# Attention with memory slots and a top-1 mixture of experts: where the expert gate is worked out

## The chip, the cores and the metric

The kernel runs on one core of a Trainium2 chip. The metric is the device time of one execution in microseconds; of several executions the median is given.

## The reference

An attention whose keys and values are first folded into 32 memory slots per head makes 4608 rows x of 512 numbers. Each row goes to the one of 8 experts with the largest logit, through a two-layer network with 1024 hidden units, and the result is scaled by a gate of two factors: the row's largest softmax probability and the sigmoid of its output logit for that expert.

```python
a = softmax(phi, over the sequence)              # 8 batches x 8 heads x 576 x 32
k_m, v_m = a^T k, a^T v                          # 32 x 64 per head
x = softmax(q k_m^T / 8) v_m                     # 4608 x 512
logits = x @ w_gate
e_idx = np.argmax(logits, axis=1)
probs = np.exp(logits - logits.max(-1)); probs /= probs.sum(-1) + 1e-9
eom = 1.0 / (1.0 + np.exp(-(x @ w_output_gate)))
for e in range(8):
    h = np.maximum(x[mask] @ w1[e], 0.0)
    out[mask] = gate_w[mask, None] * eom[mask, e, None] * (h @ w2[e])
```

The exponential of the largest logit minus itself is 1, so the gate of a row is 1 / ((sum of exp(logit - max) + 1e-9) x (1 + exp(-output logit))).

## The kernel before

**Attention and rows.** The attention runs over four pairs of batches. Each row of x goes to a scratch array `xs` in HBM as four quarters of 144 numbers: 128 values, and 16 partial logits (8 for the experts, 8 for the output gate) that belong to the two heads of that quarter. The sum of a row's four sets of 16 is its logits.

**Ranking.** Once per pair `rank` (L932) gives each row its expert and its place among the rows of that expert: maximum, comparisons, a product with a triangular matrix on TensorE (L981 to L985), and one-hot rows on GpSimd (L1014). Beside these steps it works out the gates of the pair's 1152 rows: logit minus maximum on GpSimd (L957), an exponential (L967), the chosen output logit (L966) and its sum (L973), the sum of the exponentials (L987), the exponential of the negated output logit (L988), two additions, a product, a reciprocal (L993 to L1004) and a copy to 16 columns (L1006). Four DMAs of SyncE (L1008, L1011) then write the gate over the partial logits of every quarter of the rows in `xs`. For the second pair these DMAs wait in a list and are issued from hooks. `rank` is a generator: its steps are taken one by one, among the steps of other work.

**Expert slots.** The rows of an expert are worked off in slots: five slots of three blocks of 128 rows that are gathered as whole rows (slots 0 to 4; 0 and 1 run while the attention still goes on), then nine "quart" slots, in turn of three blocks and of two (five and four of them), whose rows are gathered quarter by quarter, so that a quarter of a row lies on each group of 32 partitions. Slots of single blocks stand behind a condition on the counts and don't run with these inputs. A gather of GpSimd (L542) brings the rows into `xg` (three buffers).

`several` (L1281) computes one slot. First half: for each of 4 weight tiles u and 2 column blocks j a group of 12 matmuls (three-block slot) or 8 (two-block) into a PSUM bank, with x as a rounded part xh and a rest xl, weights split likewise; ScalarE and VectorE take each bank out. In a three-block slot these are L1307 and L1308. In a two-block slot they are a copy (ScalarE L1310), an addition (VectorE L1311), then per u a relu (ScalarE L1315) and two differences (VectorE L1318). After j = 0 and at the end of each u stands a call of `hook`, 8 in a slot. Second half: turns (u, k) of matmuls L1340, one y bank for each block k, and at the last u `finish_y` scales y by the gate on ScalarE (L1275) and scatters it (L1276).

The next slot's operands are made in the second half of the slot before, in five calls of `turn_x`, c = 0 to 4: for quart slots a transpose on VectorE (L1118), the rounded part on ScalarE (L1136) and the rest on VectorE (L1137). A slot's first group of matmuls needs all four chunks: it goes through chunk 0 to 3, with xh, xl, xh for each. Where `turn_x` has c = 0 for a quart slot, four small copies on ScalarE (L1111) also bring the gates, which lie in the gathered rows, to the partitions of y as `gx`. Whole slots take the gate from `xg` in place.

Between all this VectorE and ScalarE split weights: L587 rounds a 128x1024 tile on ScalarE, L602 makes the rest on VectorE, two tiles for every tile used up, through a ring of ten tiles in the quart slots. Instructions of an engine run in the order in which the program issues them.

Of the kernel before, what the change touches and what calls it, by code (L numbers as in the profile page):

```python
# [9 lines left out]
F32 = mybir.dt.float32  # L10
# [3 lines left out]
AF = mybir.ActivationFunctionType  # L14
# [4 lines left out]
P = 128  # L19
# [3 lines left out]
NCH = 9  # L23
# [48 lines left out]
def attention_moe(tc, phiT, kv, qT, wgo, wall, out):  # L72
# [3 lines left out]
    with contextlib.ExitStack() as ctx:  # L76
# [854 lines left out]

        def rank(bp, lg):  # L932

            t0 = bp * 2 * S
            lt = lg[:, :, 0:E]
            lo = lg[:, :, E:2 * E]
            b3 = [P, NCH, E]
            cs = slice(bp * NCH, (bp + 1) * NCH)
            lm = rt.tile([P, NCH], F32, name="lm")
            w1_ = rt.tile(b3, F32, name="w1_")  # L940
            w2_ = rt.tile(b3, F32, name="w2_")
            w3_ = rt.tile(b3, F32, name="w3_")
            pm = rt.tile([P, NCH], F32, name="pm")
            zs = rt.tile([P, NCH], F32, name="zs")
            gd = rt.tile([P, NCH], F32, name="gd")
            oc = rt.tile([P, E], F32, name="oc")
            rki = rt.tile([P, NCH], I32, name="rki")
            ri = rt.tile([P, NCH], I32, name="ri")
            row = rt.tile([P, NCH], F32, name="row", bufs=2)
            gt = rt.tile([P, NCH, XQ - P], F32, name="gt")  # L950
            oh = ohg[:, cs]
            dscb = desc[:].unsqueeze(1).to_broadcast(b3)
            lmb = lm[:].unsqueeze(2).to_broadcast(b3)
            V.tensor_reduce(lm[:], lt, axis=AX.X, op=ALU.max)
            yield
            V.tensor_tensor(w1_[:], lt, lmb, ALU.is_ge)
            G.tensor_tensor(w2_[:], lt, lmb, ALU.subtract)  # L957
            yield
            V.tensor_tensor(w1_[:], w1_[:], dscb, ALU.mult)
            yield  # L960
# [2 lines left out]
            V.tensor_tensor(oh, dscb, pm[:].unsqueeze(2).to_broadcast(b3), ALU.is_equal)  # L963
            yield
            V.tensor_reduce(oc[:], oh.rearrange("p c e -> p e c"), axis=AX.X, op=ALU.add)
            V.tensor_tensor(w3_[:], oh, lo, ALU.mult)  # L966
            A.activation(w2_[:], w2_[:], AF.Exp)  # L967
            yield
            if bp:
                V.tensor_tensor(ohcs[bp][:], ohcs[bp - 1][:], oc[:], ALU.add)  # L970
            else:
                V.tensor_copy(ohcs[bp][:], oc[:])
            V.tensor_reduce(zs[:], w3_[:], axis=AX.X, op=ALU.add)  # L973
            yield

            def rest():
                yield from take_pr()
                yield from hold(LATE["pe"])

                pr = ps_r.tile([P, NCH, E], F32, name="pr")  # L980
                T.matmul(pr[:], strict[:], oh, start=True, stop=False)  # L981
                if bp:
                    T.matmul(pr[:], ones_b[:], ohcs[bp - 1][:].unsqueeze(1).to_broadcast(b3), start=False, stop=False)
                for c in range(1, NCH):
                    T.matmul(pr[:, c:], ones_b[:], oh[:, 0:NCH - c], start=False, stop=(c == NCH - 1))  # L985
                yield
                V.tensor_reduce(gd[:], w2_[:], axis=AX.X, op=ALU.add)  # L987
                A.activation(zs[:], zs[:], AF.Exp, scale=-1.0)  # L988
                yield
                yield from hold(LATE["dve"])  # L990
                V.tensor_tensor(w1_[:], oh, pr[:], ALU.mult)
                taken.clear()
                V.tensor_scalar(gd[:], gd[:], 1e-9, None, ALU.add)  # L993
                yield
                with nc.allow_low_precision("whole numbers"):
                    V.tensor_reduce(rki[:], w1_[:], axis=AX.X, op=ALU.add)
                V.tensor_scalar(zs[:], zs[:], 1.0, None, ALU.add)
                yield
                V.tensor_scalar(ri[:], rki[:], 127, None, ALU.bitwise_and)
                V.tensor_scalar(jg[:, cs], rki[:], 7, None, ALU.arith_shift_right)  # L1000
                V.tensor_tensor(gd[:], gd[:], zs[:], ALU.mult)
                yield
                V.tensor_copy(row[:], ri[:])  # L1003
                V.reciprocal(gd[:], gd[:])  # L1004
                yield
                V.tensor_copy(gt[:], gd[:].unsqueeze(2).to_broadcast([P, NCH, XQ - P]))  # L1006
                def gates_out(b):
                    nc.sync.dma_start(  # L1008
                        xs[t0 + b * S:t0 + b * S + 512, P:XQ].rearrange("(c p) d -> p c d", p=P),
                        gt[:, 4 * b:4 * b + 4])  # L1010
                    nc.sync.dma_start(xs[t0 + b * S + 512:t0 + b * S + 576, P:XQ], gt[64 * b:64 * b + 64, 8])  # L1011

                def one_hot(c):
                    G.tensor_scalar(Aw[:, bp * NCH + c], iota_row[:], row[:, c:c + 1], None, ALU.is_equal)  # L1014

                if bp == 1 and "open" not in env:
                    kept.extend(functools.partial(gates_out, b) for b in range(2))
                    singly.extend(functools.partial(one_hot, c) for c in range(NCH))
                else:
                    for b in range(2):  # L1020
                        gates_out(b)
                    for c in range(NCH):
                        one_hot(c)
                        if c % 3 == 2:
                            yield
                ranked.append(bp)
# [71 lines left out]
        def turn_x(z, c):  # L1098
# [4 lines left out]
            if c == 0:  # L1103
                z["x"] = (mo.tile([P, 4, 3 * P], F32R, name="xh"),
                          None if nb == 2 else mo.tile([P, 4, 3 * P], F32R, name="xl"))
                if z["quart"]:
                    z["xt"] = {}
                    z["g"] = env["xt"].tile([P, 3], F32, name="gx")
                    for b in range(4):
                        k = nb - (nb == 2 and b > 1)  # L1110
                        A.copy(z["g"][32 * b:32 * b + 32, 0:k], xg[0:32, 0:k, XQ * b + P])  # L1111
            xh, xl = z["x"]
            if z["quart"]:

# [20 lines left out]
                pt = pt[:, 0:n]  # L1135
            A.copy(xh[:, c, 0:n], pt)  # L1136
            V.tensor_tensor(xl[:, c, 0:n], pt, xh[:, c, 0:n].bitcast(F32), ALU.subtract)  # L1137

        NT = 5 * NBP
        deferred = []  # L1140
# [124 lines left out]
        def finish_y(z, k, py):  # L1265
            y = mo.tile([P, DM], F32, name="y", bufs=2)
            n = P
            if (z["nb"], k) == (2, 1):

                n = 64  # L1270
                ya = env["xt"].tile([64, DM], F32, name="ya", bufs=1)
                A.copy(ya[:], py[64:128])
                V.tensor_tensor(ya[:], py[0:64], ya[:], ALU.add)
                py = ya[:]
            A.activation(y[0:n], py[0:n], AF.Copy, scale=z["g"][0:n, k:k + 1] if z["quart"] else z["xg"][:, k, P:P + 1])  # L1275
            G.indirect_dma_start(  # L1276
                out=out, out_offset=bass.IndirectOffsetOnAxis(ap=z["idx"][1][0:n, z["q0"] + k:z["q0"] + k + 1], axis=0),
                in_=y[0:n], in_offset=None, bounds_check=NTOK - 1, oob_is_err=False)

        def several(i, st, nxt, hook):  # L1280


            z = order[i]
            nb, x, h = z["nb"], z["x"], []
            n_ = nb * P
            for u in range(4):
# [34 lines left out]
                if nb == 3:  # L1321
                    st.done(PUMP[0])
                hook()
            py = [bank([DM], "ps") for _ in range(nb)]

            turns = [(u, k) for u in range(4, 8) for k in range(nb)]
# [24 lines left out]
        def single(i, st, nxt):  # L1351
# [15 lines left out]
            for u in range(4):  # L1367
# [12 lines left out]
                    turn_h(0)  # L1380
                if u < 3:
                    st.done(PUMP[1])
            for c in range(5):
                nxt(c)
            turn_h(1)
# [131 lines left out]
```

## Time and profile before

| | |
|---|---|
| median of 3 executions | 546.48 us (546.12 to 997.22) |
| the profiled execution's own time | 548.27 us |
| its span, first to last instruction | 546.5 us |
| mean granted TensorE clock | 0.974 |
| busy: TensorE, VectorE, ScalarE, GpSimd | 508.1, 353.6, 288.1, 239.5 us |
| DMA | 123.54 MB in 42062 packets, of these 10320 under 512 B |

The profiled execution took 1.8 us more than the median and 1.77 us more than its own span. The engine names in the rows are PE for TensorE, PEld for its weight loads, DVE for VectorE, ACT for ScalarE, POOL for GpSimd and SP for SyncE. Each line of the timeline has the start in us, the duration, the engine, the program's line, the operation, out<-in with shapes, the number of instructions put together, and in brackets the idle time before it with what ended it. TensorE is idle for a large part of the first 110 us and hardly at all afterwards.

### The profile page before, as it was taken

Reading aid. Unit: us, or ns where it says so; the run is one execution under the profiler, and the core shown is the slowest. Engines: PE = TensorE matmul, PEld = TensorE weight load, DVE = VectorE, ACT = ScalarE, POOL = GpSimd, SP = SyncE. Lnnn points to the kernel's source line nnn. Section 1 sums busy time; section 2 is a strip of 40 time slices with the busy share of each in tenths; the row PEclk is TensorE's granted clock in tenths of the full one; section 3 lists DMA queues with packets and bytes.
Section 4 is the critical chain, followed back from the end, with each engine's and each line's share of the span. In section 5 each row is a group of like instructions: output and inputs, shape, how many; then the busy total and the mean of one; then the engine's idle time right before and its main releaser. Section 6 shows DMA issues by size and latency. Waiting matters only on the chain. (4 is left out here: it accounts for less than half of the span.)

```text
span 546.5 us, 10564 instructions
## 1 busy us (share of the span) xinstructions
PE 508.1 (93%) x3850; PEld 438.2 (80%) x3850; DVE 353.6 (65%) x783; ACT 288.1 (53%) x536; POOL 239.5 (44%) x254
## 2 busy tenths in 40 slices
PE   3888788799999999999999999999999999999993
PEld 2555465598788898898998989998999799898982
DVE  4376979978965569888455547953875397639310
ACT  3467466754445466363443547853874476458210
POOL 2244386582625045220575554465547253721101
PEclk9969879999999999999999999999999999999998
DMA  8999998998767668745566665865785577743001
GB/s 303 418 391 388 411 347 282 365 359 299 228 191 256 196 192 280 225 147 155 155 163 205 184 228 168 257 194 202 217 257 143 187 249 232 239 135 98 30 20 44
DMA packets 42062, 123.54 MB, mean 226 GB/s; under 512 B 10320, under 2 KB 10384, under 8 KB 41616
## 3 DMA queue, kind: packets, MB, share of 16 engines
q1 hardware_dynamic: 35200, 102.71, 57.2%
q0 software_dynamic: 6800, 20.06, 10.6%
q8 instruction: 32, 0.52, 0.4%
q14 instruction: 30, 0.25, 0.1%
HBM read 102.40 MB, written 20.35 MB: 225 GB/s over the span
## 5 line engine op out<-in xcount | busy, mean ns | idle before, releaser
L1340 PE MATMUL bps<-whl,hh 128*128 128x512 f32 x640 | 192.6, 393 | 0.8 <-issue 0.8
L1303 PE MATMUL bps<-xh,whl 128*128 128x384 f32 x640 | 165.8, 336 | 0.0
L602 DVE TENSOR_TENSOR whl<-w,whl 128x1024 fp32r<-128x1024 f32 x112 | 136.4, 1222 | 9.7 <-ACT whl L587 9.3
L1340 PEld LDWEIGHTS bps<-whl,hh 128*128 128x128 f32 x640 | 119.9, 188 | 25.9 <-issue 1.6
L587 ACT CAST whl<-w 128x1024 fp32r<-128x1024 f32 x112 | 116.6, 1046 | 24.8 <-remote 14.4
L1303 PEld LDWEIGHTS bps<-xh,whl 128*128 128x128 f32 x640 | 115.8, 188 | 1.2 <-issue 0.6
L542 POOL DMA_INDIRECT xg<-xs,idx_ql x84 | 99.6, 1186 | 25.6 <-issue 22.6
L1303 PE MATMUL bps<-xl,whl 128*128 128x384 f32 x320 | 107.1, 335 | 0.0
L1340 PE MATMUL bps<-whl,hl 128*128 128x512 f32 x240 | 93.6, 390 | 0.0
L1308 DVE SCALAR_TENSOR_TENSOR hl<-bps,hh 128x384 fp32r<-128x384 f32 x80 | 43.9, 554 | 66.2 <-ACT hh L1307 51.2
L1307 ACT ACTIVATE hh<-bps 128x384 fp32r<-128x384 f32 x80 | 38.9, 493 | 78.7 <-PE bps L1303 70.5
L1276 POOL DMA_INDIRECT out<-y,idx_ol x23 | 25.8, 1122 | 108.5 <-ACT y L1275 54.4
L1303 PEld LDWEIGHTS bps<-xl,whl 128*128 128x128 f32 x320 | 60.1, 188 | 0.5
L1340 PEld LDWEIGHTS bps<-whl,hl 128*128 128x128 f32 x240 | 45.1, 188 | 8.5
L885 POOL TENSOR_TENSOR ea<-ea,mx 128x512 f32<-128x512 f32 (+1 forms) x20 | 19.3, 963 | 45.8 <-DVE mx L883 38.8
L1298 PE MATMUL bps<-xh,whl 128*128 128x384 f32 x128 | 37.7, 338 | 0.0
L1299 PE MATMUL bps<-xh,whl 128*128 128x256 f32 x128 | 35.7, 279 | 0.0
L1014 POOL TENSOR_SCALAR Aw<-iota_row,row 128x128 bf16<-128x128 bf16 x36 | 29.3, 828 | 8.3 <-DVE row L1003 8.3
L1276 POOL DMA_INDIRECT out<-y,idx_ob x9 | 10.7, 1189 | 49.0 <-ACT y L1275 39.5
L1275 ACT ACTIVATE y<-bps,gx 128x512 f32<-128x512 f32 x19 | 13.1, 688 | 35.6 <-PE bps L1340 29.0
L916 PE MATMUL bpd<-ve_b,aT 64*128 64x144 f32 (+1 forms) x320 | 27.9, 325 | 2.5 <-DVE ea L879 1.4
L879 DVE STREAM_TRANSPOSE ea<-bpd 128x512 f32<-128x512 f32 (+1 forms) x20 | 13.2, 660 | 23.7 <-PE bpd L869 11.8
(277 smaller groups left out, 599.7 us busy)
## 6 DMA issues: line engine op xcount, KB each, us to landing
w<-wall SPq DMA_DIRECT2D x112, 512.0 KB
kvt<-kv SPq DMA_DIRECT2D x32, 512.0 KB
qt<-qT SPq DMA_DIRECT2D x16, 512.0 KB
xs<-xo SPq DMA_DIRECT2D x8, 576.0 KB
ph<-phiT SPq DMA_DIRECT2D x3, 1152.0 KB
kv<-kv SPq DMA_DIRECT2D x4, 512.0 KB
xg<-xs,idx_ql POOLq DMA_INDIRECT x84
ph<-phiT SPq DMA_DIRECT2D x4, 288.0 KB
```

The lines of the kernel that those rows point to most:

```text
L542: G.indirect_dma_start(out=z["xg"][:, k, XQ * b:XQ * b + XQ], out_offset=None, in_=xs[0:z["rows"]].rearrange("t (a q) -> (t a) q", a=4), i ...
L587: A.copy(hl[:, 0], w[:])
L602: V.tensor_tensor(hl[:, 1], w[:], hl[:, 0].bitcast(F32), ALU.subtract)
L916: T.matmul(px[to:to + n, r, sl], z["aT"][h, o:o + n], ves[2 * bp + b][h, g], start=True, stop=True)
L1014: G.tensor_scalar(Aw[:, bp * NCH + c], iota_row[:], row[:, c:c + 1], None, ALU.is_equal)
L1276: G.indirect_dma_start(out=out, out_offset=bass.IndirectOffsetOnAxis(ap=z["idx"][1][0:n, z["q0"] + k:z["q0"] + k + 1], axis=0), in_=y[0:n] ...
L1298: T.matmul(pb, w[:, 0, o:o + P], x[0][:, cc], start=(cc == 0), stop=False)
L1299: T.matmul(pb[:, 0:256], w[:, 1, o:o + P], x[0][:, cc, 0:256], start=False, stop=(cc == 3))
L1303: T.matmul(pb, w[:, b, o:o + P], x[a][:, cc, 0:n_], start=(n == 0), stop=(n == 11))
L1307: A.activation(h_[:, j], pb, AF.Relu)
L1308: V.scalar_tensor_tensor(l_[:, j], pb, 0.0, h_[:, j].bitcast(F32), ALU.max, ALU.subtract)
L1340: T.matmul(py[k], a, w[:, b, DM * f:DM * f + DM], start=(u == 4 and f == 0 and n == 0), stop=(u == 7 and f == 1 and n == len(ps) - 1))
```

## The change

`rank` keeps the ranking and loses everything that belongs to the gates: per pair eight operations on VectorE, two on ScalarE, one on GpSimd and four DMAs. `xs` keeps its partial logits. A new generator `gate` is made for each slot in `several`; every hook of the first half takes one step of it before the hook's other work, and what is left is run after the last hook (`last(gen)`), ahead of the second half. In a whole slot it sums the four partial logits with one reduction and then works out the gate from the sums, on 128 partitions. In a quart slot three copies on ScalarE first bring the partial logits of three groups of 32 partitions to the fourth group's, three additions on VectorE sum them, and the gate is worked out on 32 partitions and copied to the partitions of y by four small copies on ScalarE. The expert's number comes from the table of slots. `turn_x` no longer copies gates.

```diff
         def rank(bp, lg):
...
             V.tensor_tensor(w1_[:], lt, lmb, ALU.is_ge)
-            G.tensor_tensor(w2_[:], lt, lmb, ALU.subtract)
             yield
...
             V.tensor_reduce(oc[:], oh.rearrange("p c e -> p e c"), axis=AX.X, op=ALU.add)
-            V.tensor_tensor(w3_[:], oh, lo, ALU.mult)
-            A.activation(w2_[:], w2_[:], AF.Exp)
             yield
...
-            V.tensor_reduce(zs[:], w3_[:], axis=AX.X, op=ALU.add)
...
-                V.tensor_reduce(gd[:], w2_[:], axis=AX.X, op=ALU.add)
-                A.activation(zs[:], zs[:], AF.Exp, scale=-1.0)
...
-                V.tensor_scalar(gd[:], gd[:], 1e-9, None, ALU.add)
...
-                V.tensor_scalar(zs[:], zs[:], 1.0, None, ALU.add)
...
-                V.tensor_tensor(gd[:], gd[:], zs[:], ALU.mult)
...
-                V.reciprocal(gd[:], gd[:])
...
-                V.tensor_copy(gt[:], gd[:].unsqueeze(2).to_broadcast([P, NCH, XQ - P]))
-                def gates_out(b):
-                    nc.sync.dma_start(
-                        xs[t0 + b * S:t0 + b * S + 512, P:XQ].rearrange("(c p) d -> p c d", p=P),
-                        gt[:, 4 * b:4 * b + 4])
-                    nc.sync.dma_start(xs[t0 + b * S + 512:t0 + b * S + 576, P:XQ], gt[64 * b:64 * b + 64, 8])
...
@@ turn_x
-                    z["g"] = env["xt"].tile([P, 3], F32, name="gx")
-                    for b in range(4):
-                        k = nb - (nb == 2 and b > 1)
-                        A.copy(z["g"][32 * b:32 * b + 32, 0:k], xg[0:32, 0:k, XQ * b + P])
...
+        def gate(z):
+            nb, xg, quart = z["nb"], z["xg"], z["quart"]
+            n, m = (32, 6 if nb == 2 else 4 * nb) if quart else (P, nb)
+            z["g"] = rt.tile([P, 3], F32, name="gx", bufs=2)
...
+            if quart:
+                xv = xg[:, 0:nb].rearrange("p k (b q) -> p (k b) q", b=4)[:, 0:m, P:XQ]
+                lq = env["hs"].tile([P, F], F32, name="hs")[0:32, 0:576].rearrange("p (a j l) -> p a j l", a=3, l=2 * E)
+                for a in range(1, 4):
+                    A.copy(lq[:, a - 1, 0:m], xv[32 * a:32 * a + 32])
+                    yield
+                V.tensor_tensor(ls, xv[0:32], lq[:, 0, 0:m], ALU.add)
+                V.tensor_tensor(lq[:, 1, 0:m], lq[:, 1, 0:m], lq[:, 2, 0:m], ALU.add)
+                yield
+                V.tensor_tensor(ls, ls, lq[:, 1, 0:m], ALU.add)
+            else:
+                V.tensor_reduce(ls, xg[:, 0:nb].rearrange("p k (a q) -> p k q a", a=4)[:, :, P:XQ],
+                                axis=AX.X, op=ALU.add)
+            yield
+            V.tensor_reduce(mx, ls[:, :, 0:E], axis=AX.X, op=ALU.max)
+            V.tensor_tensor(oe[:], iota_s[:, 0:E], slot[:, z["s"]:z["s"] + 1].to_broadcast([P, E]), ALU.is_equal)
+            yield
+            V.tensor_tensor(w2, ls[:, :, 0:E], mx.unsqueeze(2).to_broadcast(b3), ALU.subtract)
+            V.tensor_tensor(w3, ls[:, :, E:2 * E], oe[0:n].unsqueeze(1).to_broadcast(b3), ALU.mult)
+            yield
+            A.activation(w2, w2, AF.Exp)
+            V.tensor_reduce(zs, w3, axis=AX.X, op=ALU.add)
+            yield
+            A.activation(zs, zs, AF.Exp, scale=-1.0)
+            V.tensor_reduce(sm, w2, axis=AX.X, op=ALU.add)
+            yield
+            V.tensor_scalar(sm, sm, 1e-9, None, ALU.add)
+            V.tensor_scalar(zs, zs, 1.0, None, ALU.add)
+            V.tensor_tensor(g, sm, zs, ALU.mult)
+            if not quart:
+                V.reciprocal(z["g"][:, 0:nb], g)
+                return
+            V.reciprocal(g, g)
+            yield
+            for b in range(4):
+                k = nb - (nb == 2 and b > 1)
+                A.copy(z["g"][32 * b:32 * b + 32, 0:k], g[:, b:4 * k - 3 + b:4])
...
@@ finish_y
-            A.activation(y[0:n], py[0:n], AF.Copy, scale=z["g"][0:n, k:k + 1] if z["quart"] else z["xg"][:, k, P:P + 1])
+            A.activation(y[0:n], py[0:n], AF.Copy, scale=z["g"][0:n, k:k + 1])
...
-        def several(i, st, nxt, hook):
+        def several(i, st, nxt, hook_):
             z = order[i]
+            gen = gate(z)
+            def hook():
+                next(gen, None)
+                hook_()
...
                 hook()
+            last(gen)
             py = [bank([DM], "ps") for _ in range(nb)]
```

The order of TensorE's instructions is the same in both kernels. The place where the order changes for the prediction is the middle of a two-block slot, where its first half ends and `turn_x` for the next slot begins. On VectorE (`whl` a split weight, `hh` and `hl` the hidden values, `xt` and `xl` the next slot's operands, `gs`, `go`, `gw` the gate's) there stood before:

```order
540 L602 TENSOR_TENSOR whl<-w,whl 128x1024
541 L1318 SCALAR_TENSOR_TENSOR hh<-hl,hh 128x2x64
542 L1318 SCALAR_TENSOR_TENSOR hh<-hl,hh 128x2x128
543 L1118 STREAM_TRANSPOSE xt<-xg 128x384 x2
544 L1137 TENSOR_TENSOR xl<-xt,xh 128x384
545 L602 TENSOR_TENSOR whl<-w,whl 128x1024
```

Now there stands, at the same place:

```order
594 L1344 SCALAR_TENSOR_TENSOR hh<-hl,hh 128x2x64
595 L1344 SCALAR_TENSOR_TENSOR hh<-hl,hh 128x2x128
596 L1142 TENSOR_REDUCE gs<-go 32x6
597 L1145 TENSOR_REDUCE gs<-gw 32x6
598 L1147 TENSOR_SCALAR gs<-gs 32x6
599 L1148 TENSOR_SCALAR gs<-gs 32x6
600 L1149 TENSOR_TENSOR gs<-gs 32x6
601 L1153 RECIPROCAL gs<-gs 32x6
602 L1088 STREAM_TRANSPOSE xt<-xg 128x384 x2
603 L1107 TENSOR_TENSOR xl<-xt,xh 128x384
```

Six operations of the gate stand between the last differences of the slot and the first transposes of the next; seven more are spread over the slot's first half. On ScalarE (`gx` the gates on y's partitions) there stood before, at the same place:

```order
240 L1315 ACTIVATE hh<-hl 128x2x192
241 L587 CAST whl<-w 128x1024
242 L1111 COPY gx<-xg 32x3 x4
243 L1136 CAST xh<-xt 128x384
244 L587 CAST whl<-w 128x1024
```

and now:

```order
253 L1341 ACTIVATE hh<-hl 128x2x192
254 L587 CAST whl<-w 128x1024
255 L1141 ACTIVATE gw<-gw 32x48
256 L1144 ACTIVATE gs<-gs 32x6
257 L1157 COPY gx<-gs 32x2 x2
258 L1157 COPY gx<-gs 32x1 x2
259 L1106 CAST xh<-xt 128x384
260 L587 CAST whl<-w 128x1024
```

The four copies before were those of the next slot's gates, and their input was in the gathered rows. Those now are of the slot's own gates, and their input is VectorE's reciprocal; they still stand ahead of the next slot's first rounded part. The three copies of the partial logits are spread over the slot's first half on ScalarE.

## Rows read from the trace of the kernel before

**Rows 1.** The page, part 1: busy us, share of the span, instructions.
```profile
PE 508.1 (93%) x3850; PEld 438.2 (80%) x3850; DVE 353.6 (65%) x783; ACT 288.1 (53%) x536; POOL 239.5 (44%) x254
```

**Rows 2.** Windows: length, busy us by engine, granted clock, DMA share, GB/s.
```profile
120.00:140.00 20.00, 20.00 (x165) 16.68 (x164) 16.91 (x39) 9.09 (x16) 7.35 (x9) 1.00 0.91 314
440.00:460.00 20.00, 20.00 (x108) 18.44 (x108) 18.22 (x32) 15.86 (x30) 10.39 (x8) 1.00 0.80 247
```

**Rows 3.** What TensorE waits for, 66 to 112 us: total, times, longest.
```profile
PE bpd L916 <- DVE ea L879: 1.4, 3, 0.7
```

**Rows 4.** What TensorE waits for, 112 to 240 us.
```profile
PE bpd L916 <- DVE xl L1137: 1.1, 1, 1.1
```

**Rows 5.** What TensorE waits for, 240 us to the end.
```profile
PE bps L1340 <- issue: 0.8, 2, 0.5
```

**Rows 6.** VectorE in time, end of a two-block slot: start, us, operation.
```profile
446.26 0.62 DVE L1318 SCALAR_TENSOR_TENSOR hh<-hl,hh 128x128 fp32r<-128x128 f32 x2
446.80 1.03 DVE L1118 STREAM_TRANSPOSE xt<-xg 128x384 f32<-128x384 f32 x2
448.04 0.56 DVE L1137 TENSOR_TENSOR xl<-xt,xh 128x384 fp32r<-128x384 f32 x1 [0.21 <-ACT xh L1136]
...
452.76 0.55 DVE L1137 TENSOR_TENSOR xl<-xt,xh 128x384 fp32r<-128x384 f32 x1
```

**Rows 7.** ScalarE in time, the same slot.
```profile
445.25 0.53 ACT L1315 ACTIVATE hh<-hl 128x384 fp32r<-128x384 f32 x1 [0.47 <-DVE hl L1311]
...
446.62 0.84 ACT L1111 COPY gx<-xg 32x3 f32<-32x3 f32 x4
447.49 0.52 ACT L1136 CAST xh<-xt 128x384 fp32r<-128x384 f32 x1
```

**Rows 8.** TensorE in time, where the next slot begins.
```profile
452.72 0.33 PE L1303 MATMUL bps<-xh,whl 128*128 128x384 f32 x1
...
454.48 0.33 PE L1303 MATMUL bps<-xl,whl 128*128 128x384 f32 x1
```

**Rows 9.** Groups by line, VectorE: busy us, mean ns, idle before.
```profile
L954 DVE TENSOR_REDUCE lm<-lg 128x9 f32<-128x72 f32 x4 | 0.9, 229 | 0.1
...
L1001 DVE TENSOR_TENSOR gd<-gd,zs 128x9 f32<-128x9 f32 x4 | 0.6, 162 | 0.0
```

**Rows 10.** Groups by line, a small exponential on ScalarE.
```profile
L988 ACT ACTIVATE zs<-zs 128x9 f32<-128x9 f32 x4 | 0.8, 212 | 3.9 <-DVE zs L973 3.9
```

**Rows 11.** VectorE in time, the third ranking and slot 1's inputs.
```profile
140.76 0.16 DVE L1001 TENSOR_TENSOR gd<-gd,zs 128x9 f32<-128x9 f32 x1
140.84 0.17 DVE L1003 CAST row<-ri 128x9 f32<-128x9 int32 x1
140.96 0.22 DVE L1004 RECIPROCAL gd<-gd 128x9 f32<-128x9 f32 x1
...
142.67 0.30 DVE L1006 COPY gt<-gd 128x144 f32<-128x144 f32 x1 [0.78 <-DMA xs<-gt]
...
152.15 0.55 DVE L1137 TENSOR_TENSOR xl<-bpd,xh 128x384 fp32r<-128x384 f32 x1
```

**Rows 12.** VectorE in time, the second ranking.
```profile
95.86 0.17 DVE L993 TENSOR_SCALAR gd<-gd 128x9 f32<-128x9 f32 x1
```

**Rows 13.** TensorE in time: three starts after an idle stretch.
```profile
96.52 0.76 PE L916 MATMUL bpd<-ve_b,aT 64*128 64x144 f32 x8 [0.53 <-DVE ea L879]
...
108.14 0.94 PE L869 MATMUL bpd<-qt,kT 64*32 64x256 f32 x16 [2.27 <-ACT xo L918]
...
152.75 0.76 PE L916 MATMUL bpd<-ve_b,aT 64*128 64x144 f32 x8 [1.13 <-DVE xl L1137]
```

**Rows 14.** Windows after two of those starts, columns as in rows 2.
```profile
108.30:111.60 3.30, 3.30 (x28) 2.31 (x16) 2.44 (x3) 2.19 (x5) 3.14 (x4) 0.52 0.84 281
...
152.70:156.00 3.30, 3.25 (x20) 2.84 (x21) 1.43 (x5) 1.45 (x3) 0.54 (x1) 1.00 0.48 188
```

**Rows 15.** The page, part 5: a line of the three-block slots.
```profile
L1308 DVE SCALAR_TENSOR_TENSOR hl<-bps,hh 128x384 fp32r<-128x384 f32 x80 | 43.9, 554 | 66.2 <-ACT hh L1307 51.2
```

More of the change, by code (lines that the diff above doesn't have):

```diff
@@ L932, in rank @@
         def rank(bp, lg):
-            t0 = bp * 2 * S
             lt = lg[:, :, 0:E]
-            lo = lg[:, :, E:2 * E]
             b3 = [P, NCH, E]
@@ L940, in rank @@
             w1_ = rt.tile(b3, F32, name="w1_")
-            w2_ = rt.tile(b3, F32, name="w2_")
-            w3_ = rt.tile(b3, F32, name="w3_")
             pm = rt.tile([P, NCH], F32, name="pm")
-            zs = rt.tile([P, NCH], F32, name="zs")
-            gd = rt.tile([P, NCH], F32, name="gd")
             oc = rt.tile([P, E], F32, name="oc")
@@ L949, in rank @@
             row = rt.tile([P, NCH], F32, name="row", bufs=2)
-            gt = rt.tile([P, NCH, XQ - P], F32, name="gt")
             oh = ohg[:, cs]
@@ L1016, in rest @@
                 if bp == 1 and "open" not in env:
-                    kept.extend(functools.partial(gates_out, b) for b in range(2))
                     singly.extend(functools.partial(one_hot, c) for c in range(NCH))
                 else:
-                    for b in range(2):
-                        gates_out(b)
                     for c in range(NCH):
@@ L1137, in turn_x @@
             V.tensor_tensor(xl[:, c, 0:n], pt, xh[:, c, 0:n].bitcast(F32), ALU.subtract)
+        def gate(z):
+            nb, xg, quart = z["nb"], z["xg"], z["quart"]
+            n, m = (32, 6 if nb == 2 else 4 * nb) if quart else (P, nb)
+            z["g"] = rt.tile([P, 3], F32, name="gx", bufs=2)
+            tl, mm = (env["xt"], 12) if quart else (rt, 3)
+            ls, w2, w3 = (tl.tile([n, mm, w], F32, name=nm, bufs=1)[:, 0:m]
+                          for nm, w in (("gl", 2 * E), ("gw", E), ("go", E)))
+            sm_ = tl.tile([n, 4, mm], F32, name="gs", bufs=1)
+            mx, sm, zs, g = (sm_[:, i, 0:m] for i in range(4))
+            oe = rt.tile([P, E], F32, name="oe")
+            b3 = [n, m, E]
+            if quart:
[35 more added lines that the diff above has]
+                A.copy(z["g"][32 * b:32 * b + 32, 0:k], g[:, b:4 * k - 3 + b:4])
@@ L1382, in single @@
                     st.done(PUMP[1])
+            last(gate(z))
             for c in range(5):
```

## The prediction

> **What bounds the kernel now.** I read the busy shares first: TensorE works for 508.1 of 546.5 us, VectorE for 65% of the span and ScalarE for 53% [rows 1]. That says that TensorE is the bound on average, not where. The windows of 20 us show TensorE busy for the whole window in 120 to 140 and again in 440 to 460, and that the second is a tight one: VectorE is busy for 18.22 of the same 20 us [rows 2]. Then come the waits of TensorE by stretch. Between 66 and 112 us it waits 1.4 us, in three pieces, for the transposition `ea` on VectorE [rows 3]; from 112 to 240 us there is one of 1.1 us for `xl` on VectorE [rows 4]; after 240 us only 0.8 us, in which nothing in the profile was late [rows 5]. So a time saved on any other engine is worth at most these few microseconds, and a time added is free until it makes TensorE wait. Last I looked for the place with the least slack, in the timelines of the three engines. It is where a two-block slot meets the three-block slot behind it, four times in the program and alike each time.
>
> **The slack at that place.** Up to there VectorE runs without a pause longer than 0.21 us; its last piece of the next slot's inputs starts at 452.76 and ends at 453.31 [rows 6]. TensorE begins the next slot at 452.72 and comes to the first matmul that needs this piece (the eleventh, xl of chunk 3) at 454.48 [rows 8]. The slack is 454.48 - 453.31 = 1.17 us. Everything that the change puts on VectorE or in its chain with ScalarE ahead of 452.76 in such a slot pushes the piece back one for one; beyond 1.17 us TensorE stands still.
>
> **Part 1: what a two-block slot's gate adds.**
> - Three copies of partial logits on ScalarE. Their nearest row is the four small gate copies of before, 0.84 us, 0.21 each [rows 7]. They stand between the copies out of the PSUM banks, for which VectorE waits. That loop has a wait of 0.47 us in it, but for VectorE's result [rows 7], so it is no reserve. I count 3 x 0.2 = 0.6 us.
> - Seven small operations on VectorE during the first half (three sums, maximum, comparison, difference, product). A small operation lasts 162 ns, a small reduction 229 ns [rows 9], but in a row they start 0.08 us apart, or 0.12 where one needs the one before [rows 11]. Most of the seven need the one before, and some are larger: 7 x 0.13 = 0.9 us.
> - The end, in one piece behind the last differences. Before, these end at 446.26 + 0.62 = 446.88, and the first rounded part starts on ScalarE at 447.49, with the four gate copies already over by 447.46 [rows 6, 7]. Now the copies need the reciprocal. From 446.88: a reduction 0.23, the exponential 0.21 [rows 10], addition 0.16, product 0.16, reciprocal 0.22 [rows 9, 11], then four copies 0.84: 1.82 us, so 448.70 in place of 447.49, 1.2 us later. The sum over exponentials and the other addition run beside the exponential.
>
> Together 0.6 + 0.9 + 1.2 = 2.7 us, less 1.17 us of slack is 1.5 us of standstill, four times: **+6.1 us**. Lower end: 7 x 0.08 for the first half and 6 x 0.08 for the end, with ScalarE's copies beside VectorE's work, is 1.0 us, below the slack: 0. Upper end: all at full duration and one after the other, 7 x 0.229 for VectorE, 3 x 0.21 for ScalarE, and at the end 2 x 0.229 + 3 x 0.16 + 0.22 + 2 x 0.21 + 0.84 = 2.4 us in place of the 0.6 us from 446.88 to 447.49: together 1.6 + 0.6 + 1.8 = 4.0 us, less 1.17, times four: 11.5 us. I stay between the two, since rows 11 show operations that overlap in part, and a chain through two engines has no overlap.
>
> [...]
>
> **Part 2: the same gate elsewhere.** In the five three-block quart slots and the five whole slots TensorE gives the other engines more time: VectorE was idle for 66.2 us before the 80 operations of L1308, 51.2 us of it waiting for ScalarE's part of the same bank, which waits for TensorE's matmuls [rows 15]. Some 12 to 13 operations at 0.13 us, 1.6 us a slot, go into that idle time: 0. The ten slots hold these 80 operations, so each has 66.2 / 10 = 6.6 us of it; without it the ten gates would cost up to 16 us. Slots 0 and 1 are the exception, with the attention beside them; there VectorE has 20.00 - 16.91 = 3.1 us free in 20 [rows 2], and the gate's 1.6 us fit in.
>
> **Part 3: what the rankings lose.** Eight VectorE operations per pair, some 8 x 0.13 = 1 us. In the third ranking one of them also held VectorE for 0.78 us, at 142.67, waiting for the gate stores of the ranking before [rows 11]. The piece `xl` at 152.15 [rows 11] for which TensorE waits 1.13 us until 152.75 [rows 13] comes behind all that on the same engine, and 1.0 + 0.78 us is more than 1.13: this wait goes, **-1.1 us**. In the second ranking operations of the gate stand on VectorE right ahead of the `ea` for which TensorE waits 0.53 us until 96.52; the last is L993 at 95.86 [rows 12, 13]: gone as well, **-0.5 us**. What is late next behind both is ScalarE's part, which the change hardly touches. Bounds: 0, if the slots' gates take back what the rankings give, and -2.5 us, if all of the 1.4 us in rows 3 and the 1.1 us in rows 4 go. The four operations on GpSimd, eight on ScalarE and the sixteen DMAs of SyncE go from engines and queues for which TensorE waits nowhere in rows 4 and 5, and the 2.27 us until 108.14 [rows 13] are for an output copy of the attention, which stays: 0 for these.
>
> **Sum.** 6.1 - 1.1 - 0.5 = +4.5 us. On the profiled execution's own 548.27 us (its span of 546.5 and 1.77 us around it) that is 552.8; the median is 1.8 us lower, so I predict 546.48 + 4.5 = **551.0 us**, 0.8% slower.
>
> **Rivals.**
> - *The gate is hidden in the two-block slots as well.* It decides at a delay of 1.17 us per slot; the lower end of part 1 gives 1.0. For it: small operations start as close as 0.08 us [rows 11]. Against it: the chain of 1.2 us at the slot's end alone is as long as the slack. Then only the gain of part 3 remains: 546.48 - 1.6 = 544.9 us, not slower.
> [...]
> - *Every small operation costs its full duration.* The upper end of part 1, with the gain of part 3: 546.48 + 11.5 - 1.6 = 556.4 us. For it: ScalarE and VectorE hand over to each other three times in the gate's end. Against it: rows 11.
>
> **How the numbers follow.** My forecast gets 0.60, with its own range of 548 to 554.5; the hidden gate 0.22; the clock 0.10; the full price 0.08. The range for 8 in 10 takes in most of the hidden case and the clock at its middle: 544.5 to 557.5. A difference of 2%, 10.9 us, is about what a measurement of this kernel can tell from no change; the bounds are 535.6 and 557.4. Beyond the upper one lie half of the clock's case and of the full price's, 0.05 + 0.04: 0.09. Nothing in the sum reaches 10.9 us of gain, since all the waits of TensorE that the change could end are 2.5 us: 0.01. The rest is 0.90.
>
> **What would show it.** In the changed kernel's profile, TensorE should wait four times, some 1.5 us each, in the first group of the three-block slots behind the two-block ones, for the last `xl` on VectorE; the first rounded part should start some 1.2 us later behind the last differences than the 0.6 us of before; the waits at 96.52 and 152.75 should be gone; no wait should appear inside the first half of any slot. It would be wrong if those four waits are missing (hidden gate), if the granted clock falls behind them, if a whole slot or a three-block one waits for its gate in `finish_y`, or if the largest change lies before 112 us, where all the engines share the attention.

## The result, and the profile after

The changed kernel takes 553.93 us (median of 6 executions, 552.58 to 555.66), the kernel before beside it 546.58 us (median of 6): 7.3 us more, a ratio of 1.0133 with a 95% interval of 1.011 to 1.0156. The direction and the range of the prediction hold; its +4.5 us was too small by 2.9 us. The trace below is of an execution of 552.58 us with a span of 550.9 us.

The busy times of the page, as in [rows 1]:

```profile
PE 506.4 (92%) x3850; PEld 435.9 (79%) x3850; DVE 375.8 (68%) x923; ACT 300.3 (55%) x583; POOL 244.9 (44%) x250
```

TensorE works 1.7 us less than before and VectorE 22 us more. The added work is only a pointer, as the prediction said: what counts is where TensorE waits. Here are its waits from 112 to 240 us, and then from 240 us to the end, as in [rows 4, 5]:

```profile
PE bpd L916 <- DVE xl L1107: 1.1, 1, 1.1
```

```profile
PE bps L1329 <- DVE xl L1107: 4.0, 8, 0.8
PE pr L237 <- DVE bwl L229: 1.2, 1, 1.2
```

The wait of 1.1 us for `xl`, which was to go, is still there. After 240 us two waits are new: eight pieces for `xl`, two at each of the four places where a three-block slot follows a two-block one, and 1.2 us for `bwl`, which nothing in the prediction speaks of.

The start of each slot, taken from the first matmul of its first half in each trace, shows what these waits cost. A three-block slot's first half behind a two-block slot takes:

| slot behind a two-block slot | before: start, second half | after: start, second half | longer by |
|---|---|---|---|
| first | 348.51, 365.18: 16.67 us | 347.90, 366.15: 18.25 us | 1.58 us |
| second | 399.99, 416.66: 16.67 us | 400.96, 419.31: 18.35 us | 1.68 us |
| third | 452.72, 469.38: 16.66 us | 454.12, 472.39: 18.27 us | 1.61 us |
| fourth | 504.20, 520.87: 16.67 us | 507.20, 525.55: 18.35 us | 1.68 us |

That is 6.55 us in all, where the wait rows of the matmuls say 4.0. Here is TensorE in the first of these slots, as in [rows 8].

```profile
347.90 0.33 PE L1329 MATMUL bps<-xh,whl 128*128 128x384 f32 x1
...
349.52 0.45 PE L1329 MATMUL bps<-xl,whl 128*128 128x384 f32 x1 [0.24 <-DVE xl L1107]
...
351.13 0.45 PE L1329 MATMUL bps<-xl,whl 128*128 128x384 f32 x1 [0.75 <-DVE xl L1107]
```

The eleventh matmul, xl of chunk 3, comes 3.23 us after the slot's first one; before, it came 1.76 us after it [rows 8]. Of these 1.47 us the two brackets name 0.99 (0.24 and 0.75). The rows of TensorE's weight loads (PEld) name nearly all of the 6.55 us. Here is their wait after 240 us, then the loads of the two matmuls that waited, and the load of the eleventh matmul in the kernel before:

```profile
PEld bps L1329 <- DVE xl L1107: 6.3, 8, 1.0
```

```profile
349.52 0.19 PEld L1329 LDWEIGHTS bps<-xl,whl 128*128 128x128 f32 x1 [0.56 <-DVE xl L1107]
...
351.13 0.19 PEld L1329 LDWEIGHTS bps<-xl,whl 128*128 128x128 f32 x1 [1.01 <-DVE xl L1107]
```

```profile
454.31 0.19 PEld L1303 LDWEIGHTS bps<-xl,whl 128*128 128x128 f32 x1
```

Before, the eleventh matmul's load ran 0.17 us ahead of the matmul (454.31 and 454.48). Now the load waits for `xl` as well and starts together with its matmul, at 351.13, and that lead is lost. So the piece was early by 454.31 - 453.31 = 1.00 us, and not by the 1.17 us up to the matmul. The distance of the slots is the safest reading. In the two-block slot before it, VectorE and ScalarE look like this, as in [rows 6] and [rows 7]:

```profile
336.37 1.22 DVE L602 TENSOR_TENSOR whl<-w,whl 128x1024 fp32r<-128x1024 f32 x1
...
338.04 0.24 DVE L1127 TENSOR_TENSOR gl<-xg,hs 32x96 f32<-32x96 f32 x1
...
342.83 0.60 DVE L1344 SCALAR_TENSOR_TENSOR hh<-hl,hh 128x128 fp32r<-128x128 f32 x2
343.37 0.18 DVE L1142 TENSOR_REDUCE gs<-go 32x6 f32<-32x48 f32 x1
343.48 0.18 DVE L1145 TENSOR_REDUCE gs<-gw 32x6 f32<-32x48 f32 x1
343.69 0.16 DVE L1147 TENSOR_SCALAR gs<-gs 32x6 f32<-32x6 f32 x1
343.82 0.16 DVE L1148 TENSOR_SCALAR gs<-gs 32x6 f32<-32x6 f32 x1
344.01 0.15 DVE L1149 TENSOR_TENSOR gs<-gs 32x6 f32<-32x6 f32 x1
344.20 0.18 DVE L1153 RECIPROCAL gs<-gs 32x6 f32<-32x6 f32 x1
344.58 1.04 DVE L1088 STREAM_TRANSPOSE xt<-xg 128x384 f32<-128x384 f32 x2 [0.20 <-DMA xg<-xs,idx_ql]
...
350.52 0.55 DVE L1107 TENSOR_TENSOR xl<-xt,xh 128x384 fp32r<-128x384 f32 x1
```

```profile
335.08 0.27 ACT L1125 COPY hs<-xg 32x96 f32<-32x96 f32 x1
...
344.42 0.80 ACT L1157 COPY gx<-gs 32x2 f32<-32x2 f32 x4 [0.63 <-DVE gs L1153]
345.25 0.51 ACT L1106 CAST xh<-xt 128x384 fp32r<-128x384 f32 x1
```

From the two-block slot's own start (329.44 after, 434.27 before) the last `xl` ends 21.63 us later, in place of 19.04 us: 2.59 us of delay, where 2.7 had been forecast. The last differences end at 343.43, 13.99 us into the slot in place of 12.61, so 1.38 us come before the slot's end; from there the first rounded part on ScalarE starts 1.82 us later (345.25), in place of 0.61, so the end adds 1.21 us, where 1.2 had been forecast.

The 1.38 us can be split. The three copies stand in the first two of the slot's four periods, the operations on VectorE in the last two. In the kernel before, the split of a tile behind the second period's additions stands here:

```profile
440.39 1.22 DVE L602 TENSOR_TENSOR whl<-w,whl 128x1024 fp32r<-128x1024 f32 x1
```

It starts 6.12 us into the slot there and 6.93 us into it now (336.37). So 0.81 us belong to the three copies on ScalarE and the other 0.57 us to the seven operations on VectorE.

The granted clock in windows around the pause at 351.13, with the columns of [rows 2], stays at 1.00:

```profile
350.00:352.00 2.00, 1.25 (x7) 0.99 (x7) 2.00 (x3) 1.98 (x3) 0.31 (x1) 1.00 0.59 182
352.00:354.00 2.00, 2.00 (x13) 2.00 (x12) 1.93 (x3) 1.19 (x3) 1.10 (x1) 1.00 0.86 248
```

### The profile page after: what moved, and what is told of

Same layout as the page of the kernel before. It is cut to its first block, busy times and chain, and to the rows that moved or that the text cites. A ratio compares the mean times of both kernels' runs of the same rounds, so it can differ in the third digit from the quotient of the medians.

```text
span 550.9 us, 10693 instructions
## 1 busy us (share of the span) xinstructions
PE 506.4 (92%) x3850; PEld 435.9 (79%) x3850; DVE 375.8 (68%) x923; ACT 300.3 (55%) x583; POOL 244.9 (44%) x250
## 5 line engine op out<-in xcount | busy, mean ns | idle before, releaser
L542 POOL DMA_INDIRECT xg<-xs,idx_ql x84 | 107.8, 1284 | 25.6 <-issue 24.7
L1329 PE MATMUL bps<-xl,whl 128*128 128x384 f32 x320 | 108.5, 339 | 4.0 <-DVE xl L1107 4.0
L1296 POOL DMA_INDIRECT out<-y,idx_ol x23 | 24.1, 1049 | 109.2 <-ACT y L1295 59.6
L1295 ACT ACTIVATE y<-bps,gx 128x512 f32<-128x512 f32 x34 | 23.4, 687 | 65.8 <-PE bps L1367 39.6
L916 PE MATMUL bpd<-ve_b,aT 64*128 64x144 f32 (+1 forms) x320 | 25.6, 308 | 2.6 <-DVE ea L879 1.4
```

Of the source, the lines that this page charges most:

```text
L542: G.indirect_dma_start(out=z["xg"][:, k, XQ * b:XQ * b + XQ], out_offset=None, in_=xs[0:z["rows"]].rearrange("t (a q) -> (t a) q", a=4), i ...
L916: T.matmul(px[to:to + n, r, sl], z["aT"][h, o:o + n], ves[2 * bp + b][h, g], start=True, stop=True)
L1296: G.indirect_dma_start(out=out, out_offset=bass.IndirectOffsetOnAxis(ap=z["idx"][1][0:n, z["q0"] + k:z["q0"] + k + 1], axis=0), in_=y[0:n] ...
L1329: T.matmul(pb, w[:, b, o:o + P], x[a][:, cc, 0:n_], start=(n == 0), stop=(n == 11))
```

## The experiments

Each was compared with executions of the kernel before on the same chip, whose medians were 547.4 to 548.1 us there. So the differences to that median are what is compared: the changed kernel stands at +7.3 us.

**The gates of the two-block slots moved, or left out.** In `two_early` the generator of a two-block slot's gate is made in the second half of the slot before it.

```diff
-            gen = gate(z)
+            gen = z.pop("gen", None) or gate(z)
+            gens = [gen]
...
             for step, (u, k) in enumerate(turns):
+                if step == 1 and nb == 3 and i + 1 < st.hi // 8 and order[i + 1]["nb"] == 2:
+                    gens[0] = order[i + 1]["gen"] = gate(order[i + 1])
```

> The changed kernel, with the gate of each two-block slot worked out in the second half of the three-block slot before it; the same work, moved. Theory A (the cost is TensorE's standstill behind each two-block slot, 4 x 1.6 us): the four waits for xl vanish and the median falls from 553.9 by 6.4 us to about 547.5. Rival B (the cost is the amount of work on VectorE and ScalarE, wherever it stands): 553 to 554.

Measured: 547.64 us, 0.26 above the kernel before (ratio 1.0009, 0.999 to 1.0028). In its trace no wait for `xl` is left after 240 us, and each of the four first halves takes 16.67 us again. Theory A holds: 7.1 of the 7.3 us are gone, where 6.4 had been expected. B, which asked for the amount of work, falls: all fourteen gates are still worked out here.

In `two_none` the generator of a two-block slot ends at once.

```diff
         def gate(z):
+            if z["nb"] == 2:
+                z["g"] = iota_s
+                return
```

> The changed kernel without any gate work in the two-block slots (their y is scaled by another tile, so their gates are left out). Theory A: as two_early, about 547.5, since all that is left out had been on the path only there. Rival B: the four gates are 4 of 14, so 4/14 of the 7.3 us above the kernel before, 2 us: about 552.

Measured: 547.94 us, +0.56 (1.0012, 0.9999 to 1.0026). Leaving these four gates out gives no more than moving them.

**The four gate copies behind the next slot's inputs.** `gx_late` tests my picture of the chain at the slot's end.

```diff
             V.reciprocal(g, g)
             yield
+            yield nb
...
-            last(gen)
+            while next(gen, 0) != 2:
+                if nb == 3:
+                    last(gen)
+                    break
+            gens[0] = iter(())
...
+                if step == 5 and nb == 2:
+                    last(gen)
```

> The changed kernel, with the four gate copies at the end of a two-block slot's chain moved behind the next slot's inputs; all else stays. Theory A with its arithmetic (the inputs are late by 2.6 us, of which these copies are 0.8; 1.0 to 1.17 us of that is free): the standstill falls from 1.6 to about 0.75 us, the median by 3.4 us to about 550.5. If the chain through VectorE and ScalarE hides elsewhere (rival C): no change, 553.9.

Measured: 555.05 us, +7.67 (1.0132, 1.0109 to 1.0155): nothing gained, a miss for A. TensorE's waits for `xl` after 240 us are as they were without the edit:

```profile
PE bps L1331 <- DVE xl L1107: 4.0, 8, 0.7
```

The timelines show why. On VectorE the transposes start at the same distance from the reciprocal as in the changed kernel (0.37 us here, 0.38 there), and on ScalarE the first rounded part now waits for the transposes:

```profile
347.14 0.18 DVE L1153 RECIPROCAL gs<-gs 32x6 f32<-32x6 f32 x1
347.51 1.04 DVE L1088 STREAM_TRANSPOSE xt<-xg 128x384 f32<-128x384 f32 x2 [0.20 <-DMA xg<-xs,idx_ql]
```

```profile
348.18 0.51 ACT L1106 CAST xh<-xt 128x384 fp32r<-128x384 f32 x1 [1.46 <-DVE xt L1088]
...
352.72 0.79 ACT L1158 COPY gx<-gs 32x2 f32<-32x2 f32 x4
```

It starts 0.67 us after the first transpose, exactly as in the changed kernel (345.25 and 344.58). So the copies lay beside the transposes all along: in the changed kernel they end at 344.42 + 0.80 = 345.22, just when the transposes let the rounded part start. Of two paths of one length, taking away one gains nothing. The other is VectorE's own row of operations ahead of the transposes. That was theory E, tested by `end_late`, in which five of the six operations go behind the inputs with everything after them, the copies too.

```diff
+            gens = [gen]
...
-            last(gen)
+            if nb == 3:
+                last(gen)
+            gens[0] = iter(())
...
+                if step == 5 and nb == 2:
+                    last(gen)
```

> The changed kernel; in the two-block slots the last five VectorE operations of the gate's end, the second exponential and the four gate copies stand behind the next slot's inputs. Theory E (moving the copies alone changed nothing, since the transposes on VectorE wait behind the six operations and not for the copies): inputs 0.9 to 1.0 us earlier, standstill from 1.6 to 0.6 us, 4 us off 553.9, about 550. Rival (the 0.2 us that the transposes wait for something else, and what comes before the end, decide): 553 to 554.

Measured: 551.16 us, +3.57 (1.0065, 1.0042 to 1.0087), 3.8 us less than the changed kernel's +7.3. The waits for `xl` shrink from 4.0 to 0.8 us, and the four first halves are longer than 16.67 us by 0.47 to 0.52 in place of 1.6. That is what the 1.38 us ahead of the slot's end and the one reduction left there (0.11 us, 343.37 to 343.48) leave over beyond 1.0 us of slack:

```profile
PE pr L237 <- DVE bwl L229: 1.4, 1, 1.4
PE bps L1330 <- DVE xl L1107: 0.8, 4, 0.2
```

**The copies of partial logits on GpSimd.**

```diff
-                    A.copy(lq[:, a - 1, 0:m], xv[32 * a:32 * a + 32])
+                    (G.tensor_copy if nb == 2 else A.copy)(lq[:, a - 1, 0:m], xv[32 * a:32 * a + 32])
```

> The changed kernel; in the two-block slots the three copies of partial logits are on GpSimd in place of ScalarE. In the profile the two periods of the first half with these copies are longer by 0.8 us in all. Theory A: that goes, 4 x 0.8 = 3.2 us off 553.9, about 550.7. Rival: VectorE's sums then wait for GpSimd, which is in its gathers of 1.2 us each, and the standstill grows: 554 or more.

Measured: 596.24 us, +48.7 (1.089, 1.0857 to 1.0924). The rival had the direction; its size nobody had. In one two-block slot, GpSimd and VectorE:

```profile
340.35 1.04 POOL L542 DMA_INDIRECT xg<-xs,idx_ql  x1 [0.30 <-issue]
...
346.92 1.00 POOL L542 DMA_INDIRECT xg<-xs,idx_ql  x1 [0.30 <-issue]
349.89 0.96 POOL L1125 COPY hs<-xg 32x96 f32<-32x96 f32 x3 [1.98 <-DMA xg<-xs,idx_ql]
```

```profile
350.18 0.25 DVE L1127 TENSOR_TENSOR gl<-xg,hs 32x96 f32<-32x96 f32 x1 [10.44 <-POOL hs L1125]
```

The three copies stand behind six gathers of 1.0 us with 0.3 us between each, the first of the row at 340.35 and the last at 346.92, and then GpSimd waits 1.98 us more, by the profile for a gather to land. VectorE's first sum waits 10.44 us for them, and behind it the outputs of the PSUM banks (L1337, whose next addition starts at 351.06). In four slots the waits of that line add up to 36.9 us:

```profile
DVE gl L1127 <- POOL hs L1125: 36.9, 4, 10.6
```

This kernel doesn't price the copies on ScalarE (the rows above do, with 0.81 us per slot); it shows that GpSimd's queue, with six gathers in it, is no place for something that VectorE needs soon.

**The slack, measured by itself.** `two_none`, with one addition of 128x1024 on VectorE (`delay_one`, here) or two (`delay_two`, `range(2)`) where the gate's end had stood.

```diff
             last(gen)
+            if nb == 2:
+                one = iota_s[:, 0:1].to_broadcast([P, F])
+                for _ in range(1):
+                    V.tensor_tensor(env["hs"].tile([P, F], F32, name="hs")[:], one, one, ALU.add)
```

> two_none (the two-block slots' gates are left out) with one idle addition of 128x1024 on VectorE in each two-block slot where the gate's end stood, whose result nobody needs. Like L602 it should take 1.13 to 1.22 us of VectorE. Theory A (1.17 us of slack, then one for one): next to nothing, 0 to 0.2 us per slot, within 1 us of two_none (which was 0.6 us above the kernel before, so some 548). Rival (no slack: every delay of VectorE there shows): 4 x 1.15 = 4.6 us above two_none, 552.

Measured: 548.87 us, +0.82 (1.0014, 0.9994 to 1.0034), 0.3 above two_none. The one addition, and the transposes behind it:

```profile
343.56 1.22 DVE L1357 TENSOR_TENSOR hs<-iota_s 128x1024 f32<-128x1024 f32 x1
344.69 1.03 DVE L1088 STREAM_TRANSPOSE xt<-xg 128x384 f32<-128x384 f32 x2
```

> As delay_one with two such additions, 2.3 us. Theory A: 2.3 - 1.17 = 1.1 us of standstill per slot, 4.5 us above two_none, some 552. Rival (a second reserve, in the weights' ring or the free PSUM banks, takes it up): 548.

Measured: 554.20 us, +6.15 (1.0114, 1.0081 to 1.0147), 5.6 above two_none. The two additions, the transposes and the last `xl` behind them, and TensorE's first and eleventh matmul of the next slot:

```profile
344.32 2.48 DVE L1357 TENSOR_TENSOR hs<-iota_s 128x1024 f32<-128x1024 f32 x2
346.72 1.03 DVE L1088 STREAM_TRANSPOSE xt<-xg 128x384 f32<-128x384 f32 x2
...
352.65 0.55 DVE L1107 TENSOR_TENSOR xl<-xt,xh 128x384 fp32r<-128x384 f32 x1
```

```profile
350.22 0.33 PE L1332 MATMUL bps<-xh,whl 128*128 128x384 f32 x1
...
353.26 0.45 PE L1332 MATMUL bps<-xl,whl 128*128 128x384 f32 x1 [0.75 <-DVE xl L1107]
```

One addition delays the inputs by 1.13 us (343.56 to the transposes at 344.69) and the four first halves by 0.13 to 0.18 us each. Two delay them by 2.40 us (344.32 to 346.72) and the first halves by 1.39 to 1.45 us each. So the slack is 2.40 - 1.42 = 1.0 us, as the weight loads say, and not the 1.17 read off [rows 6, 8]; beyond it every tenth counts four times. The changed kernel, with 2.59 us and 1.58 to 1.68, lies on the same line.

**Slot 3.** `both_moved` is two_early with slot 3's gate in its second half.

```diff
+            gens = [iter(()) if i == 3 else gen]
...
-            last(gen)
+            if i != 3:
+                last(gen)
...
+                if i == 3 and step in (7, 8, 9):
+                    next(gen, None)
+                    next(gen, None)
```

> two_early, and in addition slot 3's gate moved from its first half to steps 7 to 9 of its second half, behind the one-hot products for which TensorE waited 1.23 us at 250.76. Theory A: about 1.3 us below two_early, some 546.2. Rival (that wait comes from the list's own planning, not from the gate): as two_early.

Measured: 546.91 us, -0.47 (0.9985, 0.9963 to 1.0007), 0.73 below two_early, less than the 1.3 expected. In the traces the wait for `bwl` falls from 1.7 us in two_early to 0.2:

```profile
PE pr L237 <- DVE bwl L229: 0.2, 1, 0.2
```

and slot 3's second half takes 19.95 us (244.94 to 264.89) in place of 21.52 in two_early (243.29 to 264.81); before, it took 19.68 (244.23 to 263.91), and in the changed kernel 21.01 (242.38 to 263.39), 1.34 us more. In all eight traces with this gate in slot 3's first half it takes 21.0 to 21.5 us, in the four others 19.6 to 20.0. In the changed kernel, VectorE starts slot 3's gate at 232.55 (L1132), ends it at 244.32 with the reciprocal, and then comes to the last one-hot products (L229), for which TensorE waits until 250.76:

```profile
232.55 0.49 DVE L1132 TENSOR_REDUCE gl<-xg 128x48 f32<-128x192 f32 x1
...
244.32 0.18 DVE L1151 RECIPROCAL gx<-gs 128x3 f32<-128x3 f32 x1
...
249.64 1.06 DVE L229 TENSOR_TENSOR bwl<-eq,tok_hl 128x405 bf16<-128x405 bf16 x2
```

In the kernel before, the slot's first `hl` and the same products stand here:

```profile
234.04 0.56 DVE L1308 SCALAR_TENSOR_TENSOR hl<-bps,hh 128x384 fp32r<-128x384 f32 x1 [3.55 <-ACT hh L1307]
...
250.17 1.06 DVE L229 TENSOR_TENSOR bwl<-eq,tok_hl 128x405 bf16<-128x405 bf16 x2
```

The products start 23.9 us after the slot's start; before, they started 22.6 us after it. From 234.04 to 250.17 the profile of the kernel before marks no pause of VectorE: the planning of the quart slots' lists fills it there, and the gate's 1.3 us came on top. So the gate causes the wait, and moving it ends it.

**What the rankings' part is worth.** `no_gates` is the changed kernel with two_none's edit for every slot (`if True`), so it leaves out all the gates; `rank_back` is no_gates with the rankings' gate operations of before in it again, without `gates_out`.

> The changed kernel without any gate work (y is scaled by another tile: all gates are left out); the rankings stay without theirs. Theory A (part 3 of the prediction): what the rankings lose is worth 1.6 us, so 1.6 us below the kernel before, 545.8 beside its 547.4. Theory D, formed from the first four profiles (the start of slot 0 moves by up to 3 us from one execution to the next, and the wait of 1.1 us at 152 is still there): no more than 0.8 us, within the noise of the kernel before. The waits for xl and for bwl behind slot 3 should both be gone.

Measured: 547.05 us, -0.54 (0.9991, 0.9977 to 1.0006).

> As no_gates (all gates left out), but the rankings again do their gate operations on VectorE, ScalarE and GpSimd; only the sixteen stores are still missing. Theory A: the operations were what the rankings' part was worth, so 1.6 us above no_gates and level with the kernel before. Theory D: level with no_gates within 0.8 us. If the stores themselves were what counted (rival): level with no_gates, and both clearly below the kernel before.

Measured: 547.64 us, +0.05 (0.9996, 0.9977 to 1.0014), 0.6 above no_gates. Both intervals take in 1. Theory A, 1.6 us, falls: even a kernel with no gates anywhere, neither in the rankings nor in the slots, gains about half a microsecond, and by the interval 1.3 us at most. Nor do the stores count, since rank_back is without them and level with the kernel before. The wait at 152 us is there in no_gates too:

```profile
PE bpd L916 <- DVE xl L1107: 1.1, 1, 1.1
```

The changed kernel's trace shows what became of the time saved. Three pieces of `xl` on VectorE, as in [rows 11]:

```profile
140.78 0.56 DVE L1107 TENSOR_TENSOR xl<-bpd,xh 128x384 fp32r<-128x384 f32 x1 [0.92 <-ACT xh L1106]
...
143.88 0.56 DVE L1107 TENSOR_TENSOR xl<-bpd,xh 128x384 fp32r<-128x384 f32 x1 [0.49 <-ACT xh L1106]
...
150.39 0.55 DVE L1107 TENSOR_TENSOR xl<-bpd,xh 128x384 fp32r<-128x384 f32 x1
```

At 142.67 before, VectorE had waited 0.78 us for the gate stores; now, at 140.78 and 143.88, it waits 0.92 and 0.49 us for ScalarE's part of `xh`. It was idle in between either way. Behind 143.88 stands the computation of the slots' indices, which is as long as it was: from L307 to the last `xl` 6.03 us before (146.12 to 152.15) and 6.04 after (144.35 to 150.39). Counted from the start of slot 0's second half (131.47 before, 129.66 after) the `xl` for which TensorE waits starts 20.68 us in before (152.15) and 20.73 after (150.39), and slot 1 starts 23.47 and 23.52 us in.

## Why the prediction was right or wrong

**The two-block slots: right.** The +6.1 us forecast there came out at 6.55 us in the trace; taking the gates away or moving them gave 6.8 to 7.1 us (7.3 less 0.56 and 0.26). The reasoning by slack was confirmed by the two delays. Inside this term the sizes were off, and the errors mostly cancel. The three copies cost 0.81 us in place of 0.6, so 0.27 each, their whole duration. The seven operations on VectorE cost 0.57 us in place of 0.9. The end cost 1.21 us, forecast as 1.2. The slack was 1.0 us in place of 1.17, since [rows 8] show the matmul and not the weight load ahead of it: 2.59 - 1.0 = 1.6 us per slot, forecast as 1.5.

**Its chain: the right length, with a second carrier.** The step "Now the copies need the reciprocal" made the four copies the last 0.84 of the 1.82 us, and left out VectorE's own row ahead of the transposes. gx_late took them away for nothing; end_late, which takes VectorE's row away as well, gained 3.8 us. The six operations and the pause behind them take 1.21 us (343.37 to 344.58). They start 0.19 to 0.21 us apart where one needs the one before, and 0.11 or 0.13 where it doesn't; the transposes start 0.38 us behind the reciprocal, with a pause of 0.20 us that the profile puts down to a gather and that no run here explains. The prediction had 0.12 us "where one needs the one before" from [rows 11], a misreading: the reciprocal at 140.96 needs the product at 140.76, 0.20 us ahead of it, and not the cast between them. That the path through the copies and the one through the transposes both came to 1.2 us is chance.

**The other slots: wrong by 1.3 us.** Part 2 gave them 0 and named slots 0 and 1 as the only crowded ones. The step that failed is "each has 66.2 / 10 = 6.6 us of it", an average over ten slots, with "Slots 0 and 1 are the exception". In the trace of the kernel before, slot 2 has 1.2 us of this idle time and slot 3 has 3.55, all of it ahead of its first `hl` at 234.04. The planning of the lists fills VectorE there, and TensorE waits for its one-hot products: a wait of 1.23 us, in a half slot that is 1.34 us longer. By the medians moving it was worth 0.7 us.

**The rankings' part: wrong.** "1.0 + 0.78 us is more than 1.13: this wait goes" took a sum of work on an engine for its lateness. VectorE now has idle time, waiting for ScalarE, between the work saved and the piece that was late, and it swallowed the saving. By the runs the part is worth 0.5 us with an interval that holds 0, not 1.6 us; its bound of 0 was nearer. The -0.5 us ahead of 96.52 can't be seen: the start of slot 0 lies anywhere between 108.84 and 112.11 us in the nine traces (after, and every run but no_gates and rank_back) in which the program up to there is the same. In the changed kernel the waits for `ea` from 66 to 112 us still add up to 1.4 us:

```profile
PE bpd L916 <- DVE ea L879: 1.4, 2, 1.1
```

The one at 96.52 has no counterpart there, but none in rank_back either, where the operations that were to cause it are back. So its cause stays open.

**The rivals.** The hidden gate fell, with a standstill in all four places. For the clock, which the chances count with 0.10 and the range takes in at its middle, no run shows a loss at the standstills of 1.5 us, each in two pieces: the granted clock was 1.00 in both windows above, and in the changed kernel's trace also from 400.96 to 411.00, from 454.12 to 464.00 and from 507.20 to 517.00, where the other three stand. The full price was paid only by the copies on ScalarE, 0.27 us each; the seven operations on VectorE took 0.57 us, where the full price was 1.6.

**The sum** is then 6.6 to 7.1 for the two-block slots, 0.7 to 1.3 for slot 3, less 0 to 0.5: 6.8 to 8.4 us, and 7.3 was measured, by its interval 6.0 to 8.5. The +4.5 us were too small mostly by the rankings' 1.1 to 1.6 us and slot 3's 0.7 to 1.3.

**Left open.** In the one trace of the kernel before, the half slot from 416.66 to 434.27 is 1.25 us longer than its like in all other traces, with the two pauses of [rows 5] in it; whether the kernel before always has them was not tried. It is one reason why the two traces' spans differ by only 4.4 us; the other is slot 1, which starts 1.76 us earlier in the changed kernel's trace (153.18, 154.94). Whether slot 0's gate costs something isn't shown either: the slot's first half takes 19.75 us before and 20.82 after, but 20.84 in rank_back, which has no gate there, and 19.74 in two_none, which has one.

## What to carry to other kernels

When the bounding engine is busy everywhere, ask of added work on the others not how much it is but which buffer it makes late, and by how much that buffer is early now: here 1.0 us, at four places; of fourteen gates these four cost 6.6 us, slot 3's about one, and the other nine nothing that shows. Read that slack per place, not as an average over slots, and up to the weight load that waits for the buffer, not only up to its matmul (1.00 and 1.17 us here). Work that must be added goes to the stages in which the helpers wait for the bound, which here was the second half of the slot before (in the kernel before, from 365.18 to 381.54, VectorE is busy for 7.42 of TensorE's 16.36 us and ScalarE for 7.62) and gave back 7.1 of the 7.3 us. And time taken off a busy helper was worth nothing that shows here, since idle time lay between it and the next thing that someone waits for.

## What the runs showed that I had not expected

Copies of 32x96 behind the gathers in GpSimd's queue held VectorE for up to 10.6 us in a two-block slot, 36.9 us over the four; in the slot shown, six gathers of 1.0 us with 0.3 us between stand ahead of them in the queue. The first 110 us of this kernel end anywhere within 3.3 us from one trace to the next, so gains there of 1 us need many executions to be seen. And a pause's bracket at the matmuls can understate it: 0.99 us were named where the eleventh matmul was 1.47 us late and the half slot 1.58 us longer. The brackets of the weight loads name 1.57 (0.56 and 1.01).
